# Half of mm1's ff tiles of the last two chunks from Strassen's seven products

## The chip, the cores and the metric

One core of a Trainium2 chip. The metric is the device time of one execution in microseconds (us), of the slowest core, here the only one. Engines: PE is TensorE, DVE is VectorE, ACT is ScalarE, POOL is GpSimd, SP issues DMAs.

## The reference

```python
attn = softmax(mask(q @ k.T / 8)) @ v        # 8 batches, 8 heads, 576 positions, 64 dims;
                                             # 4 heads with a sliding mask, 4 with a dilated one
x = attn.transpose(0, 2, 1, 3).reshape(4608, 512)
h = x @ w_in                                 # 512 -> 2048   ("mm1")
g = maximum(h, 0) ** 2
out = g @ w_out                              # 2048 -> 512   ("mm2")
```

## The kernel before

The 4608 tokens are nine chunks of 512. Chunks 1 to 6 run between the pieces of a batch's attention; **chunks 7 and 8 stand at the end, with mm1 and mm2 alone on PE**. mm1 makes 16 tiles of ff (128 rows of h for 512 tokens), each of four matmuls of 512 columns; ACT takes the relu out of PSUM and DVE squares, two tiles at a time. mm2 already uses Strassen's scheme (in Winograd's form): seven products of half size. Four of them read `sm`, the "hidden sums" that DVE makes of g.

```python
def relu_squared(c, ffc, g, ph, rts):
    i, o = divmod(ffc, 2)
    ...
    nc.scalar.activation(rt[:, o, :], ph[:], ACTF.Relu)
    if i == NK - 1:                                   # tiles 14, 15: one by one
        nc.vector.tensor_mul(g[:, ffc, :], rt[:, o, :], rt[:, o, :])
    elif o == 1:
        nc.vector.tensor_mul(g[:, ffc - 1 : ffc + 1, :], rt, rt)

def hidden_sums(g, sm, i0, i1):                       # of tiles 0-7, then of tiles 8-15
    ...
    yield nc.vector.tensor_add(s1, a21, a22)
    yield nc.vector.tensor_sub(s2, s1, a11)
    yield nc.vector.tensor_sub(s3, a11, a21)
    yield nc.vector.tensor_sub(s4, a12, s2)

def mm1_gen(c, g, sm=None):
    for ffc in range(NFF):                            # 16 tiles
        ph = pmool.tile([P, TOKC], FP32, ...)         # one of four PSUM banks
        ... four matmuls of 512 columns ...
        relu_squared(c, ffc, g, ph, rts)
        ... from tile 8 on: one hidden sum of the first half after each tile ...

def mm2_strassen_gen(c, g, sm):
    # order of products: poa (even tiles of g), pod (odd tiles), pob (s2), poa (odd tiles),
    #                    pob (s3), poc (s1), poe (s4); 16 matmuls of 256 columns each
    ...
```

The first product, `poa`, takes the even tiles of g as weights, in order: tile 12 is the seventh weight, tile 14 the eighth.

The softmax here doesn't subtract the row's maximum and nothing guards it: scores larger than these inputs give would overflow.

Of the kernel before, what the change touches and what calls it, by code (L numbers as in the profile page):

```python
# [8 lines left out]
FP16 = mybir.dt.float16  # L9
FP32 = mybir.dt.float32  # L10
I16 = mybir.dt.int16
ALU = mybir.AluOpType
ACTF = mybir.ActivationFunctionType
P = 128
# [3 lines left out]
def kernel(  # L18
# [9 lines left out]
    nc = tc.nc  # L28

    B, H, S, D = q.shape  # L30
# [6 lines left out]
    NDM = DM // P  # L37
    NFF = DFF // P
    scale = float(1.0 / (D ** 0.5))
    TOKC = 512  # L40
    NTOKC = NTOK // TOKC
# [6 lines left out]
    PADP = P - QB  # L48
# [6 lines left out]
    const = ctx.enter_context(tc.tile_pool(name="const", bufs=1))  # L55
# [2 lines left out]
    xp = ctx.enter_context(tc.tile_pool(name="xp", bufs=4))  # L58
    gp = ctx.enter_context(tc.tile_pool(name="gp", bufs=1))
    tp = ctx.enter_context(tc.tile_pool(name="tp", bufs=1))  # L60
    osb = ctx.enter_context(tc.tile_pool(name="osb", bufs=4))
    otp = ctx.enter_context(tc.tile_pool(name="otp", bufs=3))
    papool = ctx.enter_context(tc.tile_pool(name="papool", bufs=2, space=bass.MemoryType.PSUM))
    pmool = ctx.enter_context(tc.tile_pool(name="pmool", bufs=4, space=bass.MemoryType.PSUM))
    dpool = ctx.enter_context(tc.tile_pool(name="dpool", bufs=2, space=bass.MemoryType.DRAM))
# [5 lines left out]
    xT = const.tile([P, NDM, NTOK], FP16, name="xT")  # L71
# [2 lines left out]



    QKTp = [const.tile([P, 2, PADP + S], FP16, name=f"QKTp{hp}") for hp in range(2)]
    QKTd = const.tile([P, 2, 2, KPAD + S], FP16, name="QKTd")
    QKTx = const.tile([P, 2, PADP + HH * S], FP16, name="QKTx")
    AT = const.tile([P, 8, 640], FP16, name="AT")  # L80
# [235 lines left out]
    HT = TOKC // 2  # L316
    HM = DM // 2
    NK = NFF // 2
# [19 lines left out]
    def hidden_sums(g, sm, i0, i1):  # L338
        v = g_of(g)[:, i0:i1]
        a11, a12 = v[:, :, 0, 0:HT], v[:, :, 1, 0:HT]  # L340
        a21, a22 = v[:, :, 0, HT:TOKC], v[:, :, 1, HT:TOKC]
        s1, s2, s3, s4 = (sm[:, i, i0:i1, :] for i in range(4))
# [4 lines that stand above are left out]
# [35 lines left out]
    def mm1_gen(c, g, sm=None):  # L382
        xs = xT[:, :, c * TOKC : (c + 1) * TOKC]
        rts = {}
        for ffc in range(NFF):
            ph = pmool.tile([P, TOKC], FP32, name=f"ph{c}_{ffc}", tag="pm")
            for n, dmk in enumerate((2, 3, 0, 1)):
                nc.tensor.matmul(  # L388
                    ph,
                    wi[:, dmk, ffc * P : ffc * P + P],  # L390
                    xs[:, dmk, :],
                    start=(n == 0),
                    stop=(n == NDM - 1),
                )
                if n == 1:
                    yield
            relu_squared(c, ffc, g, ph, rts)
            if sm is not None and ffc >= NFF // 2:
                if ffc == NFF // 2:
                    sums = hidden_sums(g, sm, 0, NK // 2)  # L400
                if ffc == NFF - 1:
                    sums = hidden_sums(g, sm, NK // 2, NK)
                for _ in sums:
                    if ffc < NFF - 1:
                        break
            yield

    def mm2(c, g, po, t, ffc):
        nc.tensor.matmul(  # L409
            po,  # L410
            g[:, ffc, t * P : (t + 1) * P],
            wo[:, ffc, :],
            start=(ffc == 0),
            stop=(ffc == NFF - 1),
        )
# [12 lines left out]
    def mm2_strassen_gen(c, g, sm):  # L428
        gv = g_of(g)
        T = wsum["T"]  # L430
        last = c == NTOKC - 1

        def bank(name):
            return pmool.tile([P, 2, HM], FP32, name=f"{name}{c}", tag="pm")

        def half_product(acc, lhs, rhs, t, first):
            for k in range(NK):
                nc.tensor.matmul(  # L438
                    acc,
                    lhs[:, k, t * P : (t + 1) * P],  # L440
                    rhs[:, k, :],
                    start=(first and k == 0),
                    stop=(k == NK - 1),
                    skip_group_check=True,
                )
                if k % 4 == 3 and (t, k) != (1, NK - 1):
                    yield

        def product(acc, lhs, rhs, first):
            for t in range(2):  # L450
                yield from half_product(acc[:, t, :], lhs, rhs, t, first and t == 0)

        def part(name):
            return osb.tile([P, 2, HM], FP32, name=f"{name}{c}", tag="u")

        def put(half, ot, eng, cols=slice(0, DM)):
            rows = out[c * TOKC + half * HT : c * TOKC + (half + 1) * HT, cols]
            eng.dma_start(out=rows.rearrange("(t p) m -> p t m", p=P), in_=ot[:, :, cols])  # L458

        out_eng = nc.gpsimd if c < B - 1 else nc.sync  # L460
        left, right = slice(0, HM), slice(HM, DM)
        otu = otp.tile([P, 2, DM], FP32, name=f"otu{c}", tag="ot2")
        otl = otp.tile([P, 2, DM], FP32, name=f"otl{c}", tag="ot2")
        a = bank("poa")
        yield from product(a, gv[:, :, 0, 0:HT], B11, True)
        s1 = part("s1")
        nc.scalar.copy(s1, a)
        yield
        d_ = bank("pod")
        yield from product(d_, gv[:, :, 1, HT:TOKC], T[:, 3], True)  # L470
        yield
        b_ = bank("pob")
        yield from product(b_, sm[:, 1], T[:, 1], True)
        u2 = part("u2")
        nc.vector.tensor_add(u2, b_, s1)
        yield
        yield from product(a, gv[:, :, 1, 0:HT], B21, False)
        nc.scalar.copy(otu[:, :, left], a)  # L478
        if last:
            put(0, otu, nc.sync, left)  # L480
        yield
        yield from product(b_, sm[:, 2], T[:, 2], False)
        u3 = part("u3")
        nc.vector.tensor_add(u3, b_, s1)
        nc.vector.tensor_add(otl[:, :, left], d_, u3)
        if last:
            put(1, otl, nc.sync, left)
        yield
        c_ = bank("poc")
        yield from product(c_, sm[:, 0], T[:, 0], True)  # L490

        nc.vector.tensor_add(u2, c_, u2)
        nc.vector.tensor_add(otl[:, :, right], c_, u3)  # L493
        put(1, otl, out_eng, right if last else slice(0, DM))
        yield
        if last:
            for t, eng in ((0, nc.sync), (1, nc.scalar)):
                e_ = bank(f"poe{t}_")
                yield from half_product(e_[:, 0, :], sm[:, 3], B22, t, True)
                nc.vector.tensor_add(otu[:, t, right], e_[:, 0, :], u2[:, t, :])  # L500
                r0 = c * TOKC + t * P
                eng.dma_start(out=out[r0 : r0 + P, right], in_=otu[:, t, right])
        else:
            e_ = bank("poe")
            yield from product(e_, sm[:, 3], B22, True)
            nc.vector.tensor_add(otu[:, :, right], e_, u2)
            put(0, otu, out_eng)
        yield
# [20 lines left out]
    def moe_gen(c):  # L529
        g = hidden(c)  # L530
        sm = gp.tile([P, 4, NK, HT], FP16, name=f"sm{c}", tag="sm")
        yield from mm1_gen(c, g, sm)
        yield from mm2_strassen_gen(c, g, sm)


# [6 lines left out]
    def pump(n):  # L542
        for _ in range(n):
            while pending:
                try:
                    next(pending[0])
                    break
                except StopIteration:
                    pending.pop(0)
# [430 lines left out]

    for b in range(2, B):
        pending.append(moe_gen(b - 1))
        pump(1)
        if b < B - 1:

            for i in range(2):
                nc.gpsimd.tensor_copy(hold, QKTx[:, i, PADP + HH * S - 2 : PADP + HH * S - 1])
                nc.gpsimd.tensor_copy(hold, QKTd[:, i, 1, KPAD + S - 1 :])
        if 2 < b < B - 1:
            dk = keep_qk(b + 1)  # L990
        if b == 2:
            for rows, ot in late:
                nc.gpsimd.dma_start(out=rows, in_=ot)
            dk = keep_qk(b + 1)
            for _ in weight_sums():
                pump(2)
        else:
            pump(11)
        for g in range(2):
            s_sliding_x(b, g)  # L1000
            pump(7 if b == 2 and g else 5)
        s_dilated(b, 0)
        pump(5 if b == 2 else 7)
        s_dilated(b, 1)
        if b + 1 < B:
            transpose_by_dma(dk)
        pump(1 if b == 2 else 6)
        cast_v(nc.scalar)
        if b + 1 < B:
            load_v(b + 1)  # L1010
        pump(3)
        attn_values(b, lambda: pump(2))
        pump(1000)
# [33 lines left out]
```

## Time and profile before

| | |
|---|---|
| time, median of fast runs | 306.73 us |
| span of the profiled run | 305.5 us |
| PE over chunk 7, from the chain (249.50 to 275.54) | 26.04 us |
| PE over chunk 8 (275.54 to 301.60) | 26.06 us |

Another view used here is the busy time of each engine in a stretch. These are chunk 7's mm1 and mm2 before; the columns are the stretch, its length, then busy us and (number) of PE, PE's weight loads, DVE, ACT and POOL, the granted clock (PE's clock as a share of full speed), DMA share and GB/s.

```profile
249.34:263.15 13.81, 13.81 (x66) 6.27 (x64) 7.98 (x13) 8.96 (x15) 1.45 (x2) 1.00 0.20 76
263.15:275.38 12.23, 12.23 (x114) 10.96 (x112) 6.77 (x11) 1.77 (x3) 0.00 (x0) 1.00 0.00 1
```

The chain dates a PE piece about 0.16 us later than this view and the timeline, so 249.50 there and 249.34 here are the same matmul. The other views are in the prediction below.

### The profile page before, as it was taken

Reading aid. Unit: us, or ns where it says so; the run is one execution under the profiler, and the core shown is the slowest. Engines: PE = TensorE matmul, PEld = TensorE weight load, DVE = VectorE, ACT = ScalarE, POOL = GpSimd, SP = SyncE. Lnnn points to the kernel's source line nnn. Section 1 sums busy time; section 2 is a strip of 40 time slices with the busy share of each in tenths; the row PEclk is TensorE's granted clock in tenths of the full one; section 3 lists DMA queues with packets and bytes.
Section 4 is the critical chain, followed back from the end, with each engine's and each line's share of the span. In section 5 each row is a group of like instructions: output and inputs, shape, how many; then the busy total and the mean of one; then the engine's idle time right before and its main releaser. Section 6 shows DMA issues by size and latency. Waiting matters only on the chain.

```text
span 305.5 us, 7013 instructions
## 1 busy us (share of the span) xinstructions
PE 296.3 (97%) x2898; PEld 192.8 (63%) x2898; DVE 208.8 (68%) x410; ACT 185.0 (61%) x308; POOL 48.5 (16%) x97
## 2 busy tenths in 40 slices
PE   8899998999999999999999999999999999999994
PEld 3675444444696469646964697459745974684584
DVE  4653475849966797679766977697769775843744
ACT  6466777478834893489348943894389437405610
POOL 7454013006004100320032003200100010000000
PEclk9999999999999999999999999999999999999999
DMA  8999989899899998689939983989310012003004
GB/s 175 226 213 230 233 174 203 160 232 269 210 191 219 310 170 185 217 182 198 228 111 197 216 184 123 213 184 209 117 72 0 2 61 78 2 0 137 2 0 138
DMA packets 85615, 47.89 MB, mean 157 GB/s; under 512 B 68112, under 2 KB 82896, under 8 KB 85200
## 3 DMA queue, kind: packets, MB, share of 16 engines
q1 hardware_dynamic: 76688, 27.24, 40.8%
q0 software_dynamic: 8352, 19.80, 28.9%
q8 instruction: 22, 0.36, 0.5%
q10 hardware_dynamic: 544, 0.43, 0.5%
q14 instruction: 9, 0.07, 0.1%
HBM read 39.85 MB, written 16.52 MB: 184 GB/s over the span
## 4 chain that ended last, share of the span: by engine, by line
PE 90%; ACT 3%; DMA 3%; POOL 2%; issue 1%; DVE 1%; ACTq 0%; POOLq 0%
PE ph L388 42%; PE pob L438 9%; PE poa L438 9%; PE poe L438 5%; PE poc L438 5%; PE pod L438 4%; PE po L409 4%; DMA early<-in_q_dram 3%; PE paw L776 3%; PE pav L759 2%; PE pz L675 2%; PE ps L656 1%; PE py L809 1%; PE px L791 1%; POOL early L119 1%; ACT AT L628 1%
## 5 line engine op out<-in xcount | busy, mean ns | idle before, releaser
L388 PE MATMUL ph<-xT,wi 128*128 128x512 f16 x576 | 129.8, 379 | 0.0
L354 ACT ACTIVATE rt<-ph 128x512 f16<-128x512 f32 x144 | 84.9, 601 | 36.4 <-PE ph L388 36.1
L388 PEld LDWEIGHTS <-wi 128*128 128x128 f16 x576 | 54.4, 98 | 62.4
L358 DVE TENSOR_TENSOR g<-rt 128x1024 f16<-128x1024 f16 x63 | 43.5, 691 | 47.2 <-ACT rt L354 47.0
L438 PEld LDWEIGHTS <-sm 128*128 128x128 f16 x512 | 46.9, 98 | 4.8
L438 PEld LDWEIGHTS <-g 128*128 128x128 f16 x384 | 35.9, 98 | 6.9 <-DVE g L356 1.3
L438 PE MATMUL pob<-T,sm 128*128 128x256 f16 x256 | 32.5, 272 | 0.0
L438 PE MATMUL poa<-wo,g 128*128 128x256 f16 x256 | 32.4, 273 | 0.0
L458 POOL DMA_DIRECT2D out_dram<-otl x6 | 4.6, 763 | 152.6 <-DVE otl L493 152.6
L815 ACT COPY xT<-py 128x576 f16<-128x576 f16 x16 | 10.2, 640 | 27.3 <-PE py L809 27.3
L740 DVE TENSOR_TENSOR x_d<-paw,rcp_d 72x512 f16<-72x512 f32 x32 | 22.0, 687 | 1.1
L797 ACT COPY xT<-px 128x576 f16<-128x576 f16 x16 | 10.3, 642 | 13.6 <-PE px L791 13.6
L409 PE MATMUL po<-wo,g 128*128 128x512 f16 x64 | 17.8, 379 | 0.0
L735 DVE RECIPROCAL rcp_d<-paw 72x8 f32<-72x8 f32 x32 | 6.4, 199 | 16.2 <-PE paw L776 16.2
L628 ACT ACTIVATE AT<-pz 128x576 f16<-128x576 f32 x28 | 16.6, 652 | 1.0 <-PE pz L675 0.6
L628 ACT ACTIVATE AT<-ps 128x576 f16<-128x576 f32 x28 | 16.6, 649 | 0.5
L740 DVE TENSOR_TENSOR x_p<-pav,rcp_p 96x512 f16<-96x512 f32 (+1 forms) x24 | 16.2, 676 | 0.8
L438 PE MATMUL poe<-wo,sm 128*128 128x256 f16 x128 | 16.3, 273 | 0.0
L438 PE MATMUL pod<-T,g 128*128 128x256 f16 x128 | 16.3, 272 | 0.0
L438 PE MATMUL poc<-T,sm 128*128 128x256 f16 x128 | 16.2, 272 | 0.0
L478 ACT COPY otu<-poa 128x512 f32<-128x512 f32 x8 | 4.7, 586 | 17.5 <-PE poa L438 17.5
L629 DVE TENSOR_TENSOR AT<-AT,maskd 128x576 f16<-128x576 f16 x28 | 12.2, 455 | 3.5 <-ACT AT L628 2.5
(120 smaller groups left out, 354.5 us busy)
## 6 DMA issues: line engine op xcount, KB each, us to landing
sv<-in_v_dram SPq DMA_DIRECT2D x40, 128.0 KB, 3.1
sd<-in_v_dram SPq DMA_DIRECT2D x8, 512.0 KB, 6.2
dk<-in_k_dram POOLq DMA_DIRECT2D x12, 288.0 KB, 7.0
dk<-in_q_dram POOLq DMA_DIRECT2D x12, 288.0 KB, 7.5
out_dram<-otl POOLq DMA_DIRECT2D x6, 512.0 KB, 3.3
out_dram<-otu POOLq DMA_DIRECT2D x6, 512.0 KB, 4.2
sd<-in_v_dram SPq DMA_DIRECT2D x8, 288.0 KB
wi<-in_moe_w_in_dram POOLq DMA_DIRECT2D x4, 512.0 KB, 10.3
```

What stands on the lines that cost most here:

```text
L354: nc.scalar.activation(rt[:, o, :], ph[:], ACTF.Relu)
L358: nc.vector.tensor_mul(g[:, ffc - 1 : ffc + 1, :], rt, rt)
L388: nc.tensor.matmul(ph, wi[:, dmk, ffc * P : ffc * P + P], xs[:, dmk, :], start=(n == 0), stop=(n == NDM - 1),)
L409: nc.tensor.matmul(po, g[:, ffc, t * P : (t + 1) * P], wo[:, ffc, :], start=(ffc == 0), stop=(ffc == NFF - 1),)
L438: nc.tensor.matmul(acc, lhs[:, k, t * P : (t + 1) * P], rhs[:, k, :], start=(first and k == 0), stop=(k == NK - 1), skip_group_check=True,)
L628: nc.scalar.activation(AT[:, u, 0:UW], ps[:, :, 0 : UW // 2], ACTF.Exp, scale=scale)
L629: nc.vector.tensor_mul(AT[:, u, 0:UW], AT[:, u, 0:UW], mask)
L735: nc.vector.reciprocal(rcp[0:w, 0:n], pv[:, :, :, D])
L740: nc.vector.tensor_tensor(out=x[0:w, 0:n], in0=pv[:, :, :, 0:D], in1=rcp[0:w, 0:n].unsqueeze(3).to_broadcast([w, n, HH, D]), op=ALU.mult,)
L776: nc.tensor.matmul(pav[:, e, h * (D + 2) : h * (D + 2) + D + 1], AT[:, u, off : off + P], vd[:, t, 2 * a + e, h, 0 : D + 1], start=True, s ...
L797: nc.scalar.copy(xT[:, 0:2, t0 : t0 + 288], px[:, 0:UW].rearrange("x (c t) -> x c t", c=2),)
L815: nc.scalar.copy(xT[:, 2:4, t0 : t0 + 288].rearrange("x c (i r) -> x c i r", r=DIL), py[:, 0:UW].rearrange("x (c r i) -> x c i r", c=2, r= ...
```

## The change

Intent: PE is the bound, so give it fewer columns. In chunks 7 and 8, eight of the 16 ff tiles come from two "units". A unit makes four tiles (2 x 2 blocks of weights, tokens and the 512 of the model dimension) with seven products of four matmuls of 256 columns, in place of 16 matmuls of 512. The sums of weights are made once, during chunk 2's mm1; the sums of tokens at each chunk. Some sums of products gather in a PSUM bank, since PE adds to what is there; for the others ACT copies one bank to SBUF and DVE adds another bank to it. The `orders` string gives PE's order: `p` is a plain tile, `0` and `1` the next stage of a unit, `s` a hidden sum on DVE. In this cut, tile allocations and bare `yield` lines of `unit_gen` are left out, and the comments are mine.

```diff
+    units = {NTOKC - 2: 2, NTOKC - 1: 2}
+    def w_in_sums(u):            # 4 sums of 128x512 per unit, once
+    def x_sums(c):               # 4 sums of 128x512 per chunk, in the old score tiles
...
+    def unit_gen(c, u, g):
+        def finish(x):
+            nc.scalar.activation(x, x, ACTF.Relu)
+            nc.vector.tensor_mul(x, x, x)
+        product(a, w(0, 0), x_quarter(c, 0, 0), True)
+        nc.scalar.copy(m1, a)
+        product(e, w(0, 1), x_quarter(c, 1, 0), True)
+        nc.vector.tensor_add(g1[:, :, first], e, m1)
+        yield "stage"
+        product(a, s2, t2, False)
+        nc.scalar.copy(m6, a)
+        product(d, s1, t1, True)
+        finish(g1[:, :, first])
+        yield "stage"
+        product(a, s3, t3, False)
+        nc.scalar.copy(m7, a)
+        nc.vector.tensor_add(g2[:, :, second], d, m7)
+        yield "stage"
+        product(a, w(1, 1), t4, False)
+        nc.scalar.activation(g2[:, :, first], a, ACTF.Relu)
+        product(d, s4, x_quarter(c, 1, 1), False)
+        nc.vector.tensor_mul(g2[:, :, first], g2[:, :, first], g2[:, :, first])
+        nc.vector.tensor_add(g1[:, :, second], d, m6)
+        yield "stage"
+        finish(g2[:, :, second])
+        finish(g1[:, :, second])
+    orders = {2: "p01010p10p10p1psspspsp"}
...
-    otp = ctx.enter_context(tc.tile_pool(name="otp", bufs=3))
+    otp = ctx.enter_context(tc.tile_pool(name="otp", bufs=2))
...
+        relaxed = c == NTOKC - 2   # mm2 of chunk 7: poa, pod, poa, pob, poc, pob, poe
...
+        elif b == 3:               # in place of pump(11)
+            for u in range(2):
+                for _ in w_in_sums(u):
+                    pump(1)
+            pump(3)
```

More of the change, by code (lines that the diff above doesn't have):

```diff
@@ L60 @@
     tp = ctx.enter_context(tc.tile_pool(name="tp", bufs=1))
+    kp = ctx.enter_context(tc.tile_pool(name="kp", bufs=1))
     osb = ctx.enter_context(tc.tile_pool(name="osb", bufs=4))
-    otp = ctx.enter_context(tc.tile_pool(name="otp", bufs=3))
+    otp = ctx.enter_context(tc.tile_pool(name="otp", bufs=2))
     papool = ctx.enter_context(tc.tile_pool(name="papool", bufs=2, space=bass.MemoryType.PSUM))
@@ L73 @@
     wo = wpool.tile([P, NFF, DM], FP16, name="wo")
-    QKTp = [const.tile([P, 2, PADP + S], FP16, name=f"QKTp{hp}") for hp in range(2)]
+    QKTp = [kp.tile([P, 2, PADP + S], FP16, name=f"QKTp{hp}", tag=f"k{hp}") for hp in range(2)]
     QKTd = const.tile([P, 2, 2, KPAD + S], FP16, name="QKTd")
@@ L406, in mm1_gen, with quarter @@
             yield
+    units = {NTOKC - 2: 2, NTOKC - 1: 2}
+    HU = 2 * P
+    ws = [const.tile([P, 4, 2, HU], FP16, name=f"ws{u}") for u in range(2)]
+    def w_in_sums(u):
+        def quarter(i, j):
+            f0 = 4 * P * u + HU * i
+            return wi[:, 2 * j : 2 * j + 2, f0 : f0 + HU]
+        s1, s2, s3, s4 = (ws[u][:, i] for i in range(4))
+        yield nc.vector.tensor_add(s1, quarter(1, 0), quarter(1, 1))
+        yield nc.vector.tensor_sub(s2, s1, quarter(0, 0))
+        yield nc.vector.tensor_sub(s3, quarter(0, 0), quarter(1, 0))
+        yield nc.vector.tensor_sub(s4, quarter(0, 1), s2)
@@ new lines, with x_quarter @@
+    xsums = {}
+    def x_quarter(c, j, i):
+        t0 = c * TOKC + HT * i
+        return xT[:, 2 * j : 2 * j + 2, t0 : t0 + HT]
+    def x_sums(c):
+        t = [kp.tile([P, 2, 2, HT], FP16, name=f"xs{c}_{n}", tag=f"k{n}") for n in range(2)]
+        t1, t2, t3, t4 = t[0][:, 0], t[0][:, 1], t[1][:, 0], t[1][:, 1]
+        xsums[c] = t1, t2, t3, t4
+        nc.vector.tensor_sub(t1, x_quarter(c, 0, 1), x_quarter(c, 0, 0))
+        nc.vector.tensor_sub(t2, x_quarter(c, 1, 1), t1)
+        nc.vector.tensor_sub(t3, x_quarter(c, 1, 1), x_quarter(c, 0, 1))
+        nc.vector.tensor_sub(t4, x_quarter(c, 1, 0), t2)
@@ new lines, in unit_gen, with w, product, part @@
+    def unit_gen(c, u, g):
+        t1, t2, t3, t4 = xsums[c]
+        s1, s2, s3, s4 = (ws[u][:, i] for i in range(4))
+        f0 = 4 * u
+        g1, g2 = g[:, f0 : f0 + 2, :], g[:, f0 + 2 : f0 + 4, :]
+        first, second = slice(0, HT), slice(HT, TOKC)
+        def w(i, j):
+            c0 = P * f0 + HU * i
+            return wi[:, 2 * j : 2 * j + 2, c0 : c0 + HU]
+        def product(acc, lhs, rhs, start):
+            for n in range(2):
+                for k in range(2):
+                    nc.tensor.matmul(
+                        acc[:, n, :],
+                        lhs[:, k, n * P : (n + 1) * P],
+                        rhs[:, k, :],
+                        start=(start and n == 0 and k == 0),
+                        stop=(k == 1),
+                        skip_group_check=True,
+                    )
+        def part(name):
+            return osb.tile([P, 2, HT], FP32, name=f"{name}{c}_{u}", tag="u")
+        a = papool.tile([P, 2, HT], FP32, name=f"pu{c}_{u}", tag="pa")
+        def finish(x):
+            nc.scalar.activation(x, x, ACTF.Relu)
+            nc.vector.tensor_mul(x, x, x)
+        product(a, w(0, 0), x_quarter(c, 0, 0), True)
+        m1 = part("m1")
+        nc.scalar.copy(m1, a)
+        yield
+        e = pmool.tile([P, 2, HT], FP32, name=f"pe{c}_{u}", tag="pm")
+        product(e, w(0, 1), x_quarter(c, 1, 0), True)
+        nc.vector.tensor_add(g1[:, :, first], e, m1)
+        yield "stage"
+        product(a, s2, t2, False)
+        m6 = part("m6")
+        nc.scalar.copy(m6, a)
+        yield
+        d = pmool.tile([P, 2, HT], FP32, name=f"pq{c}_{u}", tag="pm")
+        product(d, s1, t1, True)
+        finish(g1[:, :, first])
+        yield "stage"
+        product(a, s3, t3, False)
+        m7 = part("m7")
+        nc.scalar.copy(m7, a)
[3 more added lines that the diff above has]
+        nc.scalar.activation(g2[:, :, first], a, ACTF.Relu)
+        yield
+        product(d, s4, x_quarter(c, 1, 1), False)
[4 more added lines that the diff above has]
+        finish(g1[:, :, second])
@@ new lines, with mm1_units_gen @@
+    orders = {
+        2: "p01010p10p10p1psspspsp",
+    }
+    def mm1_units_gen(c, g, sm, nu):
+        if c not in xsums:
+            x_sums(c)
+        xs = xT[:, :, c * TOKC : (c + 1) * TOKC]
+        rts = {}
+        stages = [unit_gen(c, u, g) for u in range(nu)]
+        sums = hidden_sums(g, sm, 0, NK // 2)
+        ffc = 4 * nu
+        for step in orders[nu]:
+            if step == "p":
+                ph = pmool.tile([P, TOKC], FP32, name=f"ph{c}_{ffc}", tag="pm")
+                for n in range(NDM):
+                    nc.tensor.matmul(
+                        ph,
+                        wi[:, n, ffc * P : ffc * P + P],
+                        xs[:, n, :],
+                        start=(n == 0),
+                        stop=(n == NDM - 1),
+                    )
+                    if n == 1:
+                        yield
+                relu_squared(c, ffc, g, ph, rts)
+                ffc += 1
+                yield
+            elif step == "s":
+                next(sums)
+            else:
+                for what in stages[int(step)]:
+                    yield
+                    if what:
+                        break
+        assert ffc == NFF
+        for _ in sums:
+            pass
+        for _ in hidden_sums(g, sm, NK // 2, NK):
+            pass
+        yield
@@ L471, in mm2_strassen_gen, with sixth, fifth @@
         yield
-        b_ = bank("pob")
-        yield from product(b_, sm[:, 1], T[:, 1], True)
-        u2 = part("u2")
-        nc.vector.tensor_add(u2, b_, s1)
-        yield
+        def sixth():
+            b_ = bank("pob")
+            yield from product(b_, sm[:, 1], T[:, 1], True)
+            u2 = part("u2")
+            nc.vector.tensor_add(u2, b_, s1)
+            yield
+            return b_, u2
+        def fifth(u2):
+            c_ = bank("poc")
+            yield from product(c_, sm[:, 0], T[:, 0], True)
+            nc.vector.tensor_add(u2, c_, u2)
+            return c_
+        relaxed = c == NTOKC - 2
+        if not relaxed:
+            b_, u2 = yield from sixth()
         yield from product(a, gv[:, :, 1, 0:HT], B21, False)
@@ L481, in mm2_strassen_gen @@
         yield
+        if relaxed:
+            b_, u2 = yield from sixth()
+            c_ = yield from fifth(u2)
+            yield
         yield from product(b_, sm[:, 2], T[:, 2], False)
@@ L487, in mm2_strassen_gen @@
             put(1, otl, nc.sync, left)
-        yield
-        c_ = bank("poc")
-        yield from product(c_, sm[:, 0], T[:, 0], True)
-        nc.vector.tensor_add(u2, c_, u2)
+        if not relaxed:
+            yield
+            c_ = yield from fifth(u2)
         nc.vector.tensor_add(otl[:, :, right], c_, u3)
         put(1, otl, out_eng, right if last else slice(0, DM))
+        if c + 1 == NTOKC - 1:
+            x_sums(c + 1)
         yield
@@ L531, in moe_gen @@
         sm = gp.tile([P, 4, NK, HT], FP16, name=f"sm{c}", tag="sm")
-        yield from mm1_gen(c, g, sm)
+        if c in units:
+            yield from mm1_units_gen(c, g, sm, units[c])
+        else:
+            yield from mm1_gen(c, g, sm)
         yield from mm2_strassen_gen(c, g, sm)
```

## The prediction

> **What bounds the kernel now.** I read the busy table first, then the chain that ended last, then the timeline of the last two chunks, because the diff touches mm1 of chunks 7 and 8 only (plus eight weight sums in an earlier batch).
>
> ```profile
> PE 296.3 (97%) x2898; PEld 192.8 (63%) x2898; DVE 208.8 (68%) x410; ACT 185.0 (61%) x308; POOL 48.5 (16%) x97
> PE 90%; ACT 3%; DMA 3%; POOL 2%; issue 1%; DVE 1%; ACTq 0%; POOLq 0%
> ```
>
> These rows of the page give busy time and the chain's shares: TensorE (PE) is busy 97% of the span and 90% of the chain. So fewer PE columns help only as long as PE doesn't begin to wait. The chain in order of time (start, length, work) for chunks 7 and 8:
>
> ```profile
> 249.50 13.81 PE ph L388 x64
> 263.32 1.75 PE poa L438 x16
> 265.06 1.75 PE pod L438 x16
> 266.81 1.75 PE pob L438 x16
> ...
> 275.54 13.81 PE ph L388 x64
> 289.36 1.75 PE poa L438 x16
> ```
>
> The reader is to see that PE runs without a gap here: mm1 13.81 us, then seven products of 1.75 us. One matmul of 512 columns costs 13.81/64 = 0.216 us, one of 256 costs 1.75/16 = 0.109 us. The slack of the others is in the timeline of these chunks and in the groups of the window (mean ns):
>
> ```profile
> 258.80 0.69 DVE L358 TENSOR_TENSOR g<-rt 128x1024 f16<-128x1024 f16 x1 [0.31 <-ACT rt L354]
> 263.12 0.42 DVE L356 TENSOR_TENSOR g<-rt 128x512 f16<-128x512 f16 x1 [0.17 <-ACT rt L354]
> 263.35 0.60 ACT L354 ACTIVATE rt<-ph 128x512 f16<-128x512 f32 x1 [0.27 <-PE ph L388]
> 263.98 0.43 DVE L356 TENSOR_TENSOR g<-rt 128x512 f16<-128x512 f16 x1 [0.44 <-ACT rt L354]
> 264.44 0.69 DVE L343 TENSOR_TENSOR sm<-g 128x1024 f16<-128x1024 f16 x1
> 265.17 0.69 DVE L344 TENSOR_TENSOR sm<-sm,g 128x1024 f16<-128x1024 f16 x1
> 265.78 0.69 DVE L345 TENSOR_TENSOR sm<-g 128x1024 f16<-128x1024 f16 x1
> 266.38 0.68 DVE L346 TENSOR_TENSOR sm<-g,sm 128x1024 f16<-128x1024 f16 x1
> ...
> L354 ACT ACTIVATE rt<-ph 128x512 f16<-128x512 f32 x32 | 19.1, 597 | 14.6 <-PE ph L388 14.6
> L475 DVE TENSOR_TENSOR u<-pob,s 128x512 f32<-128x512 f32 x2 | 1.4, 691 | 3.2 <-PE pob L438 3.2
> L467 ACT COPY s<-poa 128x512 f32<-128x512 f32 x2 | 1.2, 586 | 2.3 <-PE poa L438 2.3
> ```
>
> From these starts: a VectorE (DVE) operation of 0.69 us lets an independent next one start after 0.61 (265.78 to 266.38) and a dependent one after 0.73 (264.44 to 265.17). For 128x512 f16 (0.43 us) I take 0.34 and 0.46, with the same overlap. The even last tile g14 is ready at 263.12 + 0.42 = 263.54. PE began mm2 at 263.15 and needs g14 as eighth weight, at 263.15 + 7 x 0.109 = 263.91. **The margin of DVE at this hand-over is only about 0.4 us**; the whole prediction turns on it.
>
> **What the Trainium skill says.** "TensorE: Matmul & The Clock Gate", section "Back-to-back issue gap", has an isolated warm gap of N/2.4 + 2.5 ns: 109 ns for 256 columns and 216 for 512. The trace agrees (109 and 216); the 131 ns for 512 that the page gives as sustained does not occur here. "VectorE: DVE Perf Modes", section "The perf-mode tier table", lets tensor_tensor run at 2x for 16-bit operands in SBUF and at 1x with any PSUM operand. The trace agrees: 128x1024 f16 from SBUF takes 691 ns, and so does 128x512 with a PSUM operand. So a unit's adds from PSUM cost as much as twice the elements elsewhere. "ScalarE: Activation LUTs", section "What ACT_TABLE_LOAD costs", has 186 + 0.833 N ns for an immediate-scale ACTIVATE, 612 ns for 512 columns, and an overlap of some 93 ns back to back. The trace has 597 ns from PSUM, and pairs of rt that take 1.09 us together, so about 0.5 from start to start; a Relu in place in SBUF is not in this trace and I take 0.6.
>
> **The change part by part.** All by chunk, for each of chunks 7 and 8.
>
> PE: eight ff tiles were 32 matmuls of 512 columns. Two units of seven products of four matmuls of 256 are 56. mm1 becomes 32 x 0.2158 + 56 x 0.1092 = 13.02 us against 13.81: **0.79 us less, 1.58 for both chunks**. This is all there is to win.
>
> ScalarE (ACT): eight relus of 0.6 go; per unit three copies out of PSUM, one relu out of PSUM and three relus in place come, 14 in all. 16 operations become 22: at 0.5 from start to start 11 us in 13. It fits, with queues.
>
> DVE: four squarings of 128x1024 go (4 x 0.61). Per unit three adds from PSUM (0.61) and four squarings of 128x512 (0.34) come. mm1 and its hidden sums then hold 17 operations at 0.61 and 10 at 0.34, 13.8 us of start-to-start time against 13.02 of PE; before it was 15 and 2, 9.8 against 13.81. The first can't start before about 2 us. So DVE must end late.
>
> How late, by the order in which the built program puts its instructions and waits, counted from the first matmul of mm1, with 0.2 us from the last matmul's issue to a reader (as at each rt):
> - PE: plain tile 8 to 0.86; the units' first stages to 2.61; second stages to 4.36; third stages and tile 9 to 6.09. The bank of each unit is copied by ACT between products; these copies end at 2.2, 3.0, 3.8, 4.9, 5.9 and 6.9, each before PE returns to the bank (2.6, 3.5, 4.4, 5.7, 6.1, 8.0). Only unit 0's last product waits, for the DVE add that ends at 6.57: a stall of 0.1. Tiles 10 to 15 follow, and PE ends mm1 at about 13.14.
> - ACT: unit 1's relu of its fourth product starts behind tile 10's relu, 8.65 to 9.25; then two relus in place, tile 11, two more in place (end 11.75), tiles 12 to 15 (12 at 11.65, 14 ends at 13.25).
> - DVE has nothing to do from 8.7 to 9.28, then in order: unit 1's squaring 0.34 and add 0.61, unit 0's two squarings 0.68, tiles 10-11 0.61, unit 1's squarings 0.34 and 0.46, sum one 0.73, sum two 0.61, tiles 12-13 0.61, sum three 0.61, g14 0.43. That is 6.03 us: **g14 is there at 15.3**; tiles 12-13 at about 14.35.
> - The first product of mm2 takes g12 as seventh and g14 as eighth weight, wanted at 13.8 and 13.9. It waits about 0.6 and then 0.9. With 0.15 for the semaphore and the unhidden weight load, the eighth matmul starts at 15.45 in place of 13.90: **1.55 us of new stall**. g15 (16.3) and the second half of the hidden sums (the one that the first sm product takes at 17.7) then arrive in time, since PE itself is late (18.2 for that product in chunk 8; in chunk 7 the new order of products puts it later still).
>
> Sum per chunk: -0.79 + 0.12 + 1.55 = +0.88; for two, +1.75.
>
> Elsewhere: the eight weight sums stand at the start of chunk 2's mm1, where DVE idles 1.0 us of every 1.7; some 3 us of work go in there over four tiles and should cost nothing. The four token sums (1.5 us) are over before the third product wants them; chunk 8's lie under mm2. Two output buffers in place of three: a buffer is written again some 20 us after its store, which takes 4 us to land. The reuse of the old score tiles costs nothing, they were last read in batch 1.
>
> So 306.73 + 1.75 = 308.5; I say 308.4.
>
> **The rivals.**
> - All of the DVE work is hidden and the gain stays: 306.73 - 1.58 = 305.1. For it: mm2 leaves DVE almost idle (about 4 us of work in 12), so its lag could be made up there; the reordering of chunk 7's products serves that. Against it: the hand-over g14 precedes mm2, and its queue is 6.0 us long from the point where it can start. Without the idle 0.6 us it would still be some 1 us late.
> - ACT sets the pace: the copies from the units' banks have margins of 0.2 to 1.1 us. If a relu in place takes 0.2 us more than I assume, PE also waits at these banks and the relus of tiles 12 to 15 come late: about 0.5 us more per chunk, 309.4.
> - The lag is about half of mine (small DVE operations overlapping more than I think): gain and stall cancel, 306.7.
>
> **Range and chances.** A tenth off all DVE times moves g14 by 0.6 us per chunk, 1.2 in all; this is most of the range. The lower end, 306.6, is gain and stall cancelling; the upper, 309.4, is ACT's delay on top. Even the rivals lie within 1% of 306.73, and 2% is 6.1 us, so within 2% gets 0.97, slower 0.02, faster 0.01.
>
> **What would show it right or wrong.** Right: in the changed profile both mm1 stretches take about 13.1 us of PE, and the first product of each mm2 takes about 3.3 us in place of 1.75, with weight loads waiting for DVE's g; the other products stay at 1.75. DVE shows almost no idle time in the last 4 us of mm1. Chunks 0 to 6 keep their times. Wrong: no gap at the first product (the first rival), waits of the units' products for ACT copies of several tenths (the second), or a chunk 2 that is longer (the weight sums weren't hidden after all).

## The result

The changed kernel takes **307.86 us** (median of 4 fast runs, 307.64 to 308.41) against 306.73 (4 runs, 306.38 to 307.37). The ratio is 1.0037, 95% interval 1.0016 to 1.0059: slower by 0.4%, and within 2%. Ratios here are the mean time of one kernel's fast runs over the mean of the other's fast runs of the same rounds, so they are not quite the ratios of the medians.

The chain in order of time after, chunk 7 from tile 10 on (start, length, work; this view leaves out the shortest pieces):

```profile
256.56 0.88 PE ph L523 x4
257.46 0.60 ACT rt L356
258.06 0.50 ACT g L497
259.00 0.60 DVE g L501
...
263.01 0.60 DVE g L360
263.61 0.60 DVE sm L347
264.61 1.16 PE poa L579 x9
265.76 1.75 PE pod L579 x16
...
276.24 0.86 PE ph L523 x4
```

Before, this chain ran from mm1 into mm2 on PE alone. Now it leaves PE after tile 10, passes two relus of ACT, and stays on DVE until 264.6; PE takes it up only with the last nine matmuls of poa. From 249.50 (the chunk's first matmul, as before) to 276.24 are 26.74 us, in place of 26.04. Chunk 8 takes 26.76 (276.24 to 303.00), in place of 26.06. Together that is 1.40 us more; the span grew by 1.1 (305.5 to 306.6). The other 0.3 lies behind PE's last product: from there to the end of the span it was 3.90 us before and is 3.60 now (more on this under the first experiment).

The same stretches by busy time:

```profile
249.34:262.45 13.11, 13.11 (x91) 8.62 (x88) 10.90 (x23) 10.83 (x21) 1.45 (x2) 1.00 0.21 80
262.45:276.08 13.63, 12.57 (x113) 10.88 (x112) 8.52 (x15) 1.88 (x4) 0.00 (x0) 1.00 0.01 2
```

mm1 is 0.70 us shorter and without a gap. mm2 is 1.40 us longer, and PE is idle for 1.06 of it; the other 0.34 is in the view, which shows the last matmul ahead of each of the two waits at 0.28 us in place of 0.109. The timeline, from DVE's idle time before unit 1's squaring to the hand-over:

```profile
258.57 0.43 DVE L500 TENSOR_TENSOR g<-g 128x512 f16<-128x512 f16 x1 [0.52 <-ACT g L497]
...
262.45 0.82 PE L579 MATMUL poa<-wo,g 128*128 128x256 f16 x6
...
262.93 0.68 DVE L360 TENSOR_TENSOR g<-rt 128x1024 f16<-128x1024 f16 x1
263.53 0.68 DVE L347 TENSOR_TENSOR sm<-g 128x1024 f16<-128x1024 f16 x1
263.67 0.10 PEld L579 LDWEIGHTS <-g 128*128 128x128 f16 x1 [0.68 <-DVE g L360]
...
264.13 0.42 DVE L358 TENSOR_TENSOR g<-rt 128x512 f16<-128x512 f16 x1
...
264.61 1.16 PE L579 MATMUL poa<-wo,g 128*128 128x256 f16 x9 [0.66 <-DVE g L358]
```

Six matmuls of poa go ahead, then PE waits for tiles 12-13 (ready at 263.61) and again for tile 14 (ready at 264.55). Between the two squarings DVE makes a hidden sum (L347) that no product takes until several microseconds later.

### The profile page after: what moved, and what is told of

Its sections match the earlier page's. It is cut to its first block, busy times and chain, and to the rows that moved or that the text cites. A ratio compares the mean times of both kernels' runs of the same rounds, so it can differ in the third digit from the quotient of the medians.

```text
span 306.6 us, 7160 instructions
## 1 busy us (share of the span) xinstructions
PE 295.3 (96%) x2946; PEld 197.1 (64%) x2946; DVE 222.0 (72%) x446; ACT 188.8 (62%) x320; POOL 48.8 (16%) x97
## 4 chain that ended last, share of the span: by engine, by line
PE 78%; DMA 11%; DVE 4%; ACT 4%; SPq 1%; issue 1%; POOL 0%; ACTq 0%; POOLq 0%
PE ph L390 28%; PE pob L579 9%; PE poa L579 9%; DMA sq<-in_k_dram 7%; PE poe L579 5%; PE poc L579 5%; PE pod L579 4%; PE po L550 3%; DMA wi<-in_moe_w_in_dram 3%; PE paw L938 2%; PE pu L457 2%; PE pav L921 2%; PE ph L523 2%; PE pz L837 1%; PE ps L818 1%; PE py L971 1%
## 5 line engine op out<-in xcount | busy, mean ns | idle before, releaser
L390 PE MATMUL ph<-xT,wi 128*128 128x512 f16 x448 | 101.8, 379 | 0.0
L356 ACT ACTIVATE rt<-ph 128x512 f16<-128x512 f32 x128 | 74.9, 602 | 31.8 <-PE ph L390 21.5
L390 PEld LDWEIGHTS <-wi 128*128 128x128 f16 x448 | 41.9, 98 | 47.7
L360 DVE TENSOR_TENSOR g<-rt 128x1024 f16<-128x1024 f16 x55 | 38.0, 691 | 33.5 <-ACT rt L356 33.3
L579 PE MATMUL poa<-wo,g 128*128 128x256 f16 x256 | 33.1, 273 | 2.1 <-DVE g L358 1.3
L523 PE MATMUL ph<-xT,wi 128*128 128x512 f16 x64 | 15.1, 379 | 0.0
```

Source lines behind the costliest of these rows:

```text
L390: nc.tensor.matmul(ph, wi[:, dmk, ffc * P : ffc * P + P], xs[:, dmk, :], start=(n == 0), stop=(n == NDM - 1),)
L523: nc.tensor.matmul(ph, wi[:, n, ffc * P : ffc * P + P], xs[:, n, :], start=(n == 0), stop=(n == NDM - 1),)
L579: nc.tensor.matmul(acc, lhs[:, k, t * P : (t + 1) * P], rhs[:, k, :], start=(first and k == 0), stop=(k == NK - 1), skip_group_check=True,)
```

## The experiments

The theory (A): PE's saving is real, and what takes it back is DVE, which is late with tiles 12 to 14 because its added work and three hidden sums stand ahead of them. The rivals: (B) ACT's queue, or the units' PSUM banks that ACT must empty, holds PE; (C) the loss is in the other parts of the change. Nine runs were made; all gave correct results. They are called, in the order of the sections below, no_units, one_chunk, late_sums, late_sums_strict, two_sums, stt, split_sums, and in the last section split_relaxed and split_again.

### The other parts without the units

```diff
-    units = {NTOKC - 2: 2, NTOKC - 1: 2}
+    units = {}
```

> The changed kernel with no chunk taking units: weight sums in chunk 2, token tiles' pool, two output buffers, chunk 7's relaxed order and chunk 8's token sums stay, mm1 of chunks 7 and 8 is the plain one. Theory A: these cost nothing, 306.7 us (within 0.3 of before). Rival C: the loss is in these parts, 307.5 us or more.

Measured 306.53 us against 306.85 (ratio 0.9985, interval 0.9971 to 0.9999); the PE time of the two chunks is 26.04 and 26.05 us. The weight sums, the pools and the new order of chunk 7's products cost nothing. C falls. If anything the other parts gain a little, since the interval lies just below 1. The traces suggest where: in the eight with the old order of products in the last chunk, this one among them, the span ends 3.55 to 3.64 us after PE's last product, and 3.90 in the kernel before, where SP's last store took 0.84 us to issue in place of 0.42. There is only one trace of the kernel before, so what causes this is not shown.

### Units in chunk 7 alone

```diff
-    units = {NTOKC - 2: 2, NTOKC - 1: 2}
+    units = {NTOKC - 2: 2}
```

> Units in chunk 7 only. Theory A: the loss is local to each chunk, 0.70 us in chunk 7 by the trace, none in chunk 8: about 307.4 us by the trace's sum, 307.3 by half of the measured difference. If the chunks interact (chunk 7's lag carried into chunk 8), it is 306.7 or 307.9.

Measured 307.35 us against 306.85 (ratio 1.0016, interval 1.0000 to 1.0031). The time alone would not decide it, but PE takes 26.74 us over chunk 7 and 26.05 over chunk 8. The loss is 0.70 us for each chunk with units, and nothing is carried on.

### All hidden sums behind the last squaring

```diff
-        2: "p01010p10p10p1psspspsp",
+        2: "p01010p10p10p1pppp",
-        relaxed = c == NTOKC - 2
+        relaxed = c >= NTOKC - 2
```

> The changed kernel with all of chunk 7's and 8's hidden sums after the last squaring g15, and the relaxed order of products in both chunks. Theory A (DVE is late with g12 and g14 because three hidden sums and its own added work stand ahead of them): the eighth matmul of poa finds g14 ready within 0.1 us, no stall at the start of mm2, mm1 13.1 us and mm2 12.3 us, both chunks 0.7 us shorter than in the kernel before: about 305.3 us. Rival B (ACT's copies and relus, or the units' PSUM banks, hold PE): nothing of ACT is changed, so it stays at 307.9. Rival C (weight sums, fewer output buffers and so on cost it): also 307.9.

The chain of this run at the two hand-overs and at its end:

```profile
258.04 4.32 PE ph L523 x20
262.36 1.75 PE poa L579 x16
...
283.37 4.32 PE ph L523 x20
287.69 1.75 PE poa L579 x16
...
298.20 0.70 DVE u L643
```

Both poa products take 1.75 us: the stall is gone, by DVE's order alone, with every ACT and PE instruction of mm1 as it was. PE takes 25.33 us over chunk 7 (249.25 to 274.58), 0.71 less than in the kernel before. That is A against B. But the time is 306.6 us (ratio to before 0.999, interval 0.9972 to 1.0008), not 305.3: the forecast of the time missed, and the last line shows where, since the chain goes from PE's sixth product to DVE's adds and no longer through poe. This is taken up below.

### The same with the old order of products

```diff
-        2: "p01010p10p10p1psspspsp",
+        2: "p01010p10p10p1pppp",
-        relaxed = c == NTOKC - 2
+        relaxed = False
```

> As late_sums, but with the old order of the seven products in both chunks, so that the first sm product is third. Theory A: no stall at poa, but the second half of sum two ends about 18.5 us after mm1's start while the third product wants it at 17.0: a stall of about 1.5 us at pob in each chunk, in all 308.4 us. If DVE were not the limit (B or C), no such stall and no difference from late_sums.

Measured 307.7 us (ratio 1.0026, interval 1.0012 to 1.0040), 0.7 less than forecast. The stall is where it was expected, at pob, in the waits from 249 to 306 us:

```profile
PEld L579 <- DVE sm L346: 2.7, 2, 1.4
PE pob L579 <- DVE sm L346: 2.2, 2, 1.1
```

It is 1.26 us a chunk (26.59 us of PE against late_sums' 25.33), a little less than the 1.5 expected. DVE has more work than fits into mm1, and what is put last decides which product waits.

### One sum fewer ahead of tile 14

```diff
-        2: "p01010p10p10p1psspspsp",
+        2: "p01010p10p10p1pssppp",
```

> The changed kernel with sums one and two ahead of tiles 12-13 as there, but sum three behind g15. One sum of 0.61 us less ahead of g14. Theory A: g14 0.6 us earlier, the stall at poa about 0.8 us per chunk in place of 1.4, chunk 26.2 us of PE in place of 26.74; span of PE over both chunks 1.1 us less than in the changed kernel. B: no change.

PE takes 26.14 us over each of the chunks (248.77, 274.91 and, for the end of poe, 301.06), 0.60 less than with three sums; 26.2 were expected. One sum of DVE moved is its whole start-to-start time on PE.

### Relu and squaring in one DVE operation

```diff
-            nc.scalar.activation(x, x, ACTF.Relu)
-            nc.vector.tensor_mul(x, x, x)
+            nc.vector.scalar_tensor_tensor(
+                out=x, in0=x, scalar=0.0, in1=x, op0=ALU.max, op1=ALU.mult
+            )
```

> The changed kernel with each relu in place on ACT and the squaring after it on DVE made one DVE operation, max(x, 0) times x: six ACT operations fewer per chunk, the same number on DVE. Rival B (ACT's queue is what makes g14 late): g14 earlier by 1 us or more, 306.5 or less. Theory A: DVE is the queue; if the fused operation runs at one element per cycle (0.61 from start to start against 0.34), four of them ahead of g14 make it 1.1 us later per chunk: about 309.7 us; if it runs at two per cycle, within 0.3 of 307.9.

Measured 311.04 us (5 runs, 309.5 to 311.5; ratio 1.0126). ACT has twelve operations fewer in the two chunks, and the time grows, so ACT's load isn't the limit (DVE's load grew at the same time; the run that moves DVE's sums alone is the cleaner test). The fused operation's group, and the granted clock after chunk 7's stall (third column from the right):

```profile
L471 DVE SCALAR_TENSOR_TENSOR g<-g 128x512 f16<-128x512 f16 x12 | 7.7, 684 | 0.0
...
261.90:265.11 3.21, 1.11 (x9) 0.59 (x7) 3.14 (x7) 0.60 (x1) 0.00 (x0) 1.00 0.02 5
...
266.00:268.50 2.50, 2.50 (x14) 1.75 (x13) 2.44 (x4) 0.58 (x1) 0.00 (x0) 0.50 0.00 0
```

The fused operation takes 684 ns against 422 of the plain squaring (12 of them in the changed kernel), as long as a plain operation on twice the elements (687 for 128x1024): this is the slower of the two cases. Chunk 8 takes 27.72 us, 0.96 more than in the changed kernel, near the 1.1 expected for that case. Chunk 7 takes 29.36, and this was not foreseen: after a stretch of 3.2 us in which PE was busy for 1.1, its clock was at half speed for some 3.4 us (265.6 to 269.0). Chunk 8 had the same two waits (1.45 and 0.66 us) and no such drop. Three of the five runs have a mean clock of 0.994 and the fastest, 309.5 us, has 1.0, which fits that some executions have the drop and some don't; one run of 311.04 at a mean clock of 1.0 stays unexplained.

### The hidden sums in the order in which they are wanted

In late_sums DVE idles for 0.55 us ahead of tiles 12-13, waiting for ACT's relu. One sum goes there; the others follow tile 15, those that pob needs first. mm2 keeps its old order.

```diff
-        2: "p01010p10p10p1psspspsp",
+        2: "p01010p10p10p1psppp",
-        relaxed = c == NTOKC - 2
+        relaxed = False
+        rest = hidden_sums(g, sm, NK // 2, NK)
+        next(sums)          # s2 of the first half
+        next(rest)          # s1, s2 of the second half
+        next(rest)
         for _ in sums:
             pass
-        for _ in hidden_sums(g, sm, NK // 2, NK):
+        for _ in rest:
             pass
```

> The changed kernel with the old order of products in both chunks, and the hidden sums re-ordered: sum one of the first half in DVE's idle 0.55 us ahead of tiles 12-13, then, after g15, sum two of the first half, sums one and two of the second half, and only then sums three and four. Theory A: g14 at most 0.1 to 0.15 us late, sum two complete about 16.5 us after mm1's start where the third product wants its second half at 17.0, so no stall there either. Both chunks 25.4 us of PE against 26.04 before, and the end of the program as before: 305.4 to 305.6 us. If the end of late_sums was long for another reason than its order of products, the end is long here too, and the time is 306.

Measured **305.21 us** against 306.96 (5 runs, 304.94 to 305.34; ratio 0.9947, interval 0.9934 to 0.9959). The chain at chunk 7's hand-over:

```profile
257.80 4.32 PE ph L523 x20
262.12 1.82 PE poa L583 x16
263.94 1.75 PE pod L583 x16
265.69 1.75 PE pob L583 x16
```

poa is 0.07 us long of 1.75, pob waits for nothing, and PE takes 25.41 us over chunk 7 (249.01 to 274.42), as forecast. A second measurement of the same kernel is in the next experiment. This version beats both kernels. The change's own saving is 0.63 us a chunk, 1.26 in all, of the 1.75 that the medians differ by; about 0.3 is the shorter end that all traces of the changed program have, with units or without, and the rest, by elimination, lies ahead of chunk 7. 0.16 us a chunk of the 0.79 that PE's columns offer is not reached, 0.09 in mm1's one short wait and 0.07 in poa.

### The relaxed order in the last chunk

late_sums kept its PE saving but not its time. Here split_sums has the relaxed order in both chunks, on one chip with a repetition of split_sums. The second text below speaks of a second chip; by the record it was the same one as in the last experiment.

```diff
-        relaxed = False
+        relaxed = c >= NTOKC - 2
```

> split_sums with the relaxed order of products in both chunks. In late_sums PE's last product began 1.7 us earlier than before, but DVE's last operation ended only 1.15 us earlier. Theory: in the relaxed order the sixth product (sm2) is the second half of b, and three DVE adds of 0.7 us hang on it ahead of the last adds, so the last chunk ends with a DVE queue: PE's products as in split_sums, DVE's last add some 0.5 us later, 305.7 us. Rival: late_sums was slow by the noise of the program's first part, then 305.2 as split_sums.

> split_sums once more, on the same chip as split_relaxed, so that the two can be compared directly and its gain over the kernel before is measured on a second chip: 305.2 us, 0.5% less than before.

Measured 306.28 us with the relaxed order (0.6 more than forecast; ratio to before 0.9988, interval 0.9973 to 1.0003) and 305.32 without (ratio 0.9955, interval 0.9941 to 0.9969). The ends of the two, relaxed first:

```profile
298.31 0.69 DVE L647 TENSOR_TENSOR u<-pob,s 128x512 f32<-128x512 f32 x1 [1.05 <-PE pob L583]
...
299.75 0.97 SPq L603 DMA_DIRECT2D out_dram<-otl  x2
300.24 0.75 DVE L663 TENSOR_TENSOR otu<-poe,u 128x256 f32<-128x256 f32 x2
```

```profile
297.93 1.99 SPq L603 DMA_DIRECT2D out_dram<-otl  x2
...
299.43 0.97 DVE L663 TENSOR_TENSOR otu<-poe,u 128x256 f32<-128x256 f32 x2
```

The last add ends at 300.99 against 300.40. Chunk 7 began 0.08 us later in the first (249.19 against 249.11), so 0.51 us are the order's doing, the 0.5 expected: three adds that hang on the sixth product stand ahead of the last ones. The spans differ by another 0.5 us (304.6 against 303.5). The stores of otl are issued from 299.75 on in the one and from 297.93 on in the other, so the last stores crowd together in the first; that this is the other half is likely, but was not tested by itself. The order that gives DVE time in chunk 7 costs time at the end of the program. late_sums has the same end (its last add ends at 300.89, and its time is 306.6), so this is where its gain went.

## Why the prediction was right

It said 308.4 us in 306.6 to 309.4; 307.86 was measured. By its steps:

- **PE's saving.** 0.79 us a chunk less 0.12 for one short wait: mm1 13.14 us predicted, 13.11 measured (249.34 to 262.45). A matmul of 256 columns kept its 0.109 us in the units.
- **The short wait** at unit 0's last product: 0.1 predicted; the chain shows 0.53 us for that product in place of 0.44. In stt, where DVE's add ahead of it came earlier, it took 0.44.
- **DVE's queue.** Idle before unit 1's squaring, for a relu in ACT's queue: 0.6 predicted, 0.52 measured. So ACT has this share in the lag, as predicted; the rest is DVE's own work. Tile 14 ready: predicted 15.30 us after mm1's start, measured 264.55 - 249.34 = 15.21. The trace's two waits stand exactly at the seventh and eighth weight of poa.
- **The stall**: 1.55 us predicted, 1.40 measured (poa from 262.45 to 265.60, 3.15 in place of 1.75). This is the term that was mis-sized: I added 0.15 us from DVE's end to the eighth matmul, and it was 0.06 (264.55 to 264.61), 0.09 less; the DVE queue was 0.09 faster than assumed; and PE, 0.03 earlier at the end of mm1, waited 0.03 longer.
- **Sum by chunk**: +0.88 predicted, +0.70 in the trace. By time +1.13 us in all, against +1.75 predicted and +1.40 of PE in the trace. The 0.35 between +1.75 and +1.40 is about twice the stall's 0.15 and mm1's 0.03. The 0.3 between +1.40 and +1.1 is the shorter end behind PE's last product, which the prediction didn't foresee and which the changed program has even without units: against no_units (306.53 us, in other rounds) the changed kernel is 1.33 us slower.
- **The parts said to cost nothing** cost nothing: no_units has the PE time of before in both chunks.
- **The rivals**: PE never waited for ACT's copies (the 0.1 us was DVE's add); the case without a stall doesn't come of itself, and comes when the sums are re-ordered. The prediction said that even without DVE's idle 0.6 us tile 14 would still be late. That is true of the order as written, but it did not say that three of the sums in the queue could go behind it, which removes the stall. A reader of the queue should have asked that.

## What to carry to other kernels

When one engine is the bound and a change gives it less to do by giving others more, draw up the others' queues at the next hand-over: the saving counts only if the last thing the bound engine waits for is not later than before by more than the saving. The order of a queue counts as well as its length: here the same operations, with the sums placed by when each is wanted, turned 0.70 us lost per chunk into 0.63 gained. And look at the very end by itself, since a reordering that is free in the middle can put work behind the last product.

## What the Trainium skill lacked or had wrong

- "TensorE: Matmul & The Clock Gate", sections "Why this matters for your kernels" and "What's actually happening": it warns of idle gaps above about 3 us, and has the clock drop after an idle window of about 3.4. In stt the granted clock fell to 0.50 for some 3.4 us after two waits of 1.45 and 0.66 us with one matmul between them (PE busy for 1.1 of 3.2 us), in one chunk and not in the other. In the changed kernel's trace, after waits of 0.40 and 0.66 us in each chunk, it did not fall. What is lacking is a figure for several short waits close together.
- The same page, section "Back-to-back issue gap": the isolated gap (216 ns for 512 columns, 109 for 256) is what a stream of weight loads and matmuls shows here (0.216 and 0.109 us); the sustained 131 ns for 512 does not occur.
- "VectorE: DVE Perf Modes", section "The perf-mode tier table": scalar_tensor_tensor has no row. On 16-bit operands in SBUF it took 684 ns for 128x512, against 422 for tensor_tensor, so it runs at 1x.
- The same page, section "The DRAIN you can't avoid": in its measurement of copies a semaphore after each operation costs nothing extra; it gives no figure for an operation that needs the result of the one just before. In the kernel before, a tensor_tensor of 0.69 us let an independent one start after 0.61 us and one that needs its result after 0.73.
- "ScalarE: Activation LUTs", section "What ACT_TABLE_LOAD costs": 186 + 0.833 N ns would be 612 for 512 columns. The relus in place in SBUF took 634 ns (12 of them), from PSUM 597; the page has one figure for both.
